# The transformed second MLP matrix of a transformer block: its column sums taken one step earlier, all six pairs staged through one ring of buffers, and the third block's x rows loaded earlier

## The chip, the cores and the metric

One core of a Trainium2 chip runs the whole program. The metric is device microseconds of one execution; lower is better. TensorE is called PE here and its weight loads PEld; DVE is VectorE, ACT is ScalarE, POOL is GpSimd, and SP is the queue of SyncE, which in this kernel only issues DMA transfers.

## What is computed

The reference is an attention layer followed by an MLP, on x of 2048 rows by 640 columns, in float32. Only the MLP is touched by the change:

```python
h = layernorm(x) * (1 + cb) + sb          # x is already the attention's output plus the input
h = h @ w1 + b1                           # 640 -> 1728
h = max(h, 0) ** 2
x = x + gb * (h @ w2 + b2)                # 1728 -> 640
```

## The kernel before, in words

**The MLP's loops.** The 2048 rows are eight blocks j = 0 to 7 of 256 rows (two halves of 128). The 1728 columns of w1 are 14 chunks of 128 (the last of 64), taken as seven pairs n = 0 to 6. A step (j,n) computes both chunks of a pair: `up` (L1145) multiplies the transposed, normalised rows `h` of the block by the chunk of w1 (15 matmuls into PSUM), ACT adds the bias and applies max(.,0) into the tile `ft` (L1162), DVE squares it (L1163). Products run in a split form of float32: a number is a high part `hi` (an ACT copy into a narrower type) and a low part `lo` (a DVE subtraction, L88), and a product is three matmuls, hi·hi, hi·lo, lo·hi, in that order. `split_a` (L1179) makes both parts of the squared tile into `ra`. The down product of a pair runs one step later than its `up`: its first half, down(0), after the first `up` of the next step, its second half, down(1), after the second `up`. So PE always needs the `ra` of the step before: ACT's copy for the first matmul of down(0), and DVE's low part for the third.

**Two forms of the down product.** In blocks 0 and 1 (`PLAIN` = 2) `down_plain` (L1295) multiplies with w2 as it is, held in the tiles `W2` (two per pair). From block 2 on `down_pair` (L1302) uses a scheme with seven products instead of eight, which wants sums of w2's quarters: for each of six pairs the combinations a, b and c (384, 256 and 384 columns wide), and one quarter that is overwritten in place, in `W2[2n][:, :, R]`. a, b and c live in DRAM (`TD`) and are fetched again by POOL for each block through a ring of four SBUF tiles (`ring`, L1217; `t_fetch`, L1267). Each fetched tile can be fetched into a ring place only after PE has used the one before it there.

**How the sums are made, in block 1.** For a pair, `t_load` (L1222) loads its two 128-row pieces of w2 into the rows `traw`; `t_sums` (L1228) is five DVE subtractions; `t_split` (L1241) is, for a, b, c and the kept quarter, an ACT copy and a DVE subtraction each, and SP's stores of a, b and c into `TD`. Pair p is loaded at the end of step (1,p), its sums stand at the end of step (1,p+1), its split in the first half of step (1,p+2), for p up to 3. Pair 4 is split at the end of (1,6). Pair 5 has its sums and its split in (2,2), in a place of its own: the tile of `h` that block 3 will use (`tst_end`).

**What sets the order.** PE, DVE, ACT and POOL run their instructions in the order in which the code issues them (`manual_schedule`, L1428), each engine in its own order; SP's order is chosen by the scheduler. Waits are by semaphores; an engine whose next instruction waits stands still. Rows of the tag `s1` (`traw`, the x rows `xx` of later blocks, the residual rows `xr`) come from five tiles, one of which holds a chunk of w1 for good, so four take turns: a new row's load waits until the last reader of the row before it in that tile is done.

**The layer norm of the next block.** While block j runs, `layer` (L1411) prepares block j+1 in pieces, at half-steps numbered 0 to 13 (2n and 2n+1): "load" (x rows), "add" (two DVE additions and SP's stores of the sums), "ln" (six ACT pieces; GpSimd works on the statistics after the second and the fourth), and the transposes with `hfb` and `h` at the numbers 8 to 12. The tables `LN_AT0` to `LN_AT2` and `LN_AT` (L1385) give the half-step of each; `LN_AT2` is for block 3, prepared during block 2.

The steps of which the prediction speaks, in the loop of L1430: m is 7j + n - 8.

Of the kernel before, what the change touches and what calls it, by code (L numbers as in the profile page):

```python
# [8 lines left out]
F32 = mybir.dt.float32  # L9
F32R = mybir.dt.float32r  # L10
I32 = mybir.dt.int32
AF = mybir.ActivationFunctionType
# [26 lines left out]
PLAIN = 2  # L39
# [12 lines left out]
def kernel(  # L52
# [19 lines left out]
    nc = tc.nc  # L72
# [14 lines left out]
    def lo(out_lo, full, hi, eng=None):  # L87
        (eng or nc.vector).tensor_tensor(out_lo, full, hi.bitcast(F32), op=ALU.subtract)  # L88
# [28 lines left out]
    def row(tag, name):  # L117
        return (pc if tag in ("s3", "s4") else mem).tile([P, D], F32, tag=tag, name=name, bufs=BUFS[tag])
# [7 lines left out]
    def ht(name, j, at=(32, 0)):  # L126

        t = mem.tile([P, NC * 512 + (32, 96)[j % 2]], F32R, tag=f"h{j % 2}", name=name, bufs=1)
        at = at[j % 2]
        return t[:, at : at + NC * 512].rearrange("p (d s n) -> p d s n", d=NC, s=2)  # L130
# [540 lines left out]
    for t in range(2, NT - 2):  # L671
        j, i = divmod(t, 2)
# [237 lines left out]
    W1, W2 = {}, {}  # L910
# [140 lines left out]
    for j in range(NB):  # L1051
        nxt = j + 1 < NB
        b, c = 2 * j + 5, 2 * j + 6
# [86 lines left out]
    NP = NF // 2  # L1140
# [29 lines left out]
    def plain(j, n):  # L1170
        return j < PLAIN or n == NF // 2 - 1 or j == NB - 1 and n >= NF // 2 - LAST
# [27 lines left out]
    def split_s(j, n):  # L1199
        t = FT[j, n]  # L1200
        a = RS[j, n] = p3.tile([P, 2, 4, P], F32, tag="rs", name=f"rs{j}_{n}").bitcast(F32R)
        nc.scalar.activation(a[:, 0], t[:, S1 : S4 + 1], AF.Copy)
        lo(a[:, 1], t[:, S1 : S4 + 1], a[:, 0])
# [7 lines left out]
    TD = [{r: dram.tile([P, 2, m], F32, name=f"td{n}_{r}") for r, m in RINGS.items()} for n in range(NP - 1)]  # L1211
    ITEMS = [(j, n, r) for j in range(PLAIN, NB) for n in range(NP) if not plain(j, n) for r in RINGS]
    L, R = slice(0, 384), slice(384, 640)
    TR_ = {}
    RING = {}

    def ring(r, name):  # L1217

        t = p3.tile([P, 768], F32, tag="ring", name=name, bufs=4)
        return t[:, : 2 * RINGS[r]].rearrange("p (s n) -> p s n", s=2).bitcast(F32R)  # L1220

    def t_load(n):  # L1222
        TR_[n] = [row("s1", f"traw{n}_{r}") for r in range(2)]
        for r in range(2):
            f = 2 * n + r
            nc.sync.dma_start(TR_[n][r], w2[f * P : (f + 1) * P])

    def t_sums(n):  # L1228
        a, b = TR_[n]
        l, r, m = slice(0, 256), slice(384, 640), slice(256, 384)  # L1230
        if n == NP - 2:
            TR_["end"] = ht("tst_end", 1).rearrange("p d s n -> p (d s n)")
            t = TR_["end"][:, :512].rearrange("p (s n) -> p s n", s=2)
        else:
            t = ring("b", f"tst{n}_b")
        TR_[n, "b"] = t
        for o, x, y in ((a[:, l], a[:, r], a[:, l]), (t[:, 1].bitcast(F32), b[:, r], a[:, r]),
                        (b[:, r], b[:, r], a[:, l]), (b[:, m], b[:, m], a[:, m]), (b[:, l], b[:, l], b[:, r])):
            nc.vector.tensor_tensor(o, x, y, op=ALU.subtract)

    def t_split(n):  # L1241

        a, b = TR_[n]
        for r, w in (("a", a[:, L]), ("b", TR_[n, "b"][:, 1].bitcast(F32)), ("c", b[:, L]), (None, b[:, R])):
            if r == "b":
                t = TR_[n, "b"]
            elif r and n == NP - 2:
                at = 512 if r == "a" else 1280
                t = TR_["end"][:, at : at + 768].rearrange("p (s n) -> p s n", s=2)
            else:  # L1250
                t = ring(r, f"tst{n}_{r}") if r else W2[2 * n][:, :, R]
            nc.scalar.activation(t[:, 0], w, AF.Copy)
            lo(t[:, 1], w, t[:, 0])
            if r:
                nc.sync.dma_start(TD[n][r], t.bitcast(F32))


    def plain_load(n):
# [60 lines left out]
    def add_bias(j, i):  # L1319
        add(XR[j, i], XR[j, i], bb)  # L1320
# [56 lines left out]
    def prep(n):  # L1377
        p_hi(n)
        p_lo(n)
        p_load(n)  # L1380
# [3 lines left out]

    LN_AT0 = {"load": 0, "add": (2, 4), "ln": (2, 4, 6, 6, 8, 8), 10: (0, 1), 11: (2, 3), 12: (4,)}  # L1385
    LN_AT1 = {"load": 3, "add": (5, 5), "ln": (5, 6, 6, 7, 8, 8), 9: (0, 1), 11: (2, 3), 12: (4,)}
    LN_AT2 = {"load": 4, "add": (6, 6), "ln": (7, 7, 8, 8, 9, 9), 10: (0, 1), 11: (2, 3), 12: (4,)}
    LN_AT = {"load": 0, "add": (3, 4), "ln": (4, 5, 6, 6, 7, 7), 8: (0, 1), 10: (2, 3), 12: (4,)}
    PREPS = iter([0, 4] * 5 + [0, 1])

# [20 lines left out]
    def layer(j, at):  # L1411
        todo = {1: LN_AT0, PLAIN: LN_AT1, PLAIN + 1: LN_AT2}.get(j, LN_AT)
        if j == NB:
            return
        if at in todo:
            t2(j, *todo[at])
        if todo["load"] == at:
            load_x1(j)
        for i in range(2):
            if todo["add"][i] == at:  # L1420
                add_x(j, i)
        for i in range(6):
            if todo["ln"][i] == at:
                if i == 0:
                    LN2[j] = ln_pieces(XM[j], f"b{j}", XX[j])
                next(LN2[j])
# [3 lines left out]
    for j in range(NB):  # L1430
        for n in range(NP):
            down = lambda k: prev and (down_plain if plain(*prev) else down_pair)(*prev, k)
            twice = not plain(j, n)
            m = NP * j + n - NP - 1
            done = j - 1 if j and prev else None
            up(j, 2 * n)
            if prev and not plain(*prev):
                split_s(*prev)
            down(0)
            if j < PLAIN:  # L1440
                layer(j + 1, 2 * n)
            if 0 < m < NP - 2:
                t_split(m - 1)
            if m == -1:
                t_load(0)
            if (j, n) == (PLAIN, 0):
                t_fetch(4)
            if j >= PLAIN:
                layer(j + 1, 2 * n)
            prep(next(PREPS, 0))  # L1450
            if n == 0 and j:
                if j - 1 >= PLAIN:
                    first_combos(j - 1)
                else:
                    Y[j - 1] = [row("s2", f"y{j - 1}_{i}") for i in range(2)]
                for r, i, c in (("2", 0, L), ("3", 0, R)):
                    end(j - 1, r, i, c)
            if n == 1 and j:
                gate(j - 1, 0)
                if j != PLAIN:  # L1460
                    finish(j - 1, j < PLAIN)
            if n == 1 and j == PLAIN:
                finish(j - 1, 0)
            if n == 2 and j == PLAIN:
                t_sums(NP - 2)
            if n == (2 if j > PLAIN else 1) and j:
                gate(j - 1, 1)
            if n == (5, 5, 4, 3)[min(j, 3)]:
                residual(j)
            for i in range(2):  # L1470
                if n == 6 and j == 0 or n == 5 and j >= PLAIN and i == 0:
                    add_bias(j, i)
            if j == NB - 1 and n == 1:
                for k in range(NP - LAST, NP - 1):
                    plain_load(k)
            if j == NB - 1 and n == 3:
                for k in range(NP - LAST, NP - 1):
                    plain_split(k)
            if j == NB - 1 and n == NP - 2:
                for i in range(2):  # L1480
                    by_gate(Y[j][i], Y[j][i], slice(0, D))
            if j == NB - 1 and n == NP - 1:
                split_a(j, n, (0,))
                for i in range(2):
                    add(Y[j][i], Y[j][i], XR[j, i])
            up(j, 2 * n + 1)
            if j >= PLAIN and n == 0:
                down(1)
            split_a(j, n, (0, 1) if (j, n) != (NB - 1, NP - 1) else (1,))
            if twice:  # L1490
                sums(j, n)
            if j < PLAIN or n:
                down(1)
            if m == NP + 1:
                t_split(NP - 2)
            prep(next(PREPS, 0))
            if n == 0 and j:
                end(j - 1, "4", 1, L)
                end(j - 1, "x", 1, R)
            if n == (2 if j > PLAIN else 1 if j == PLAIN else 0) and j:  # L1500
                finish(j - 1, j >= PLAIN)
            layer(j + 1, 2 * n + 1)
            if 0 <= m < NP - 2:
                t_sums(m)
            if m == NP - 2:
                t_split(m - 1)
            if 0 < m + 1 < NP - 1:
                t_load(m + 1)
            if m == NP - 1:
                for i in range(2):  # L1510
                    add_bias(j - 1, i)
            if j >= PLAIN and n == 5:
                add_bias(j, 1)
            if j == NB - 1 and n == NP - LAST:
                first_combos(j)
            prev = j, n
# [60 lines left out]
```

## Time and profile before

| | |
|---|---|
| time, median of 3 runs | 789.05 us (789.01 to 789.47) |
| the profiled execution | 788.85 us, of which the profile's span is 787.1 us |
| PE, DVE, ACT, POOL busy | 98%, 74%, 56%, 16% of the span |
| block 0 of the MLP begins | about 401 us |
| blocks 1, 2, 3, 4 begin (first `up`) | 448.92, 497.46, 546.82, 593.48 us |
| DMA in the stretch 495 to 543 us | 285 GB/s, engines busy 0.89 of the time |
| DMA in the stretch 590 to 636.6 us | 209 GB/s, engines busy 0.70 of the time |

A row of the timeline has the start, the duration, the engine, the source line, the operation, the tiles written and read, the shape and the number of merged instructions; at its end, in brackets, the idle time of the engine just before it and what ended that. Matmuls overlap, so a row of matmuls can end after the next one starts; the time from one row's start to the next's is what the row costs. The same holds, less strongly, on DVE and ACT. The profiled execution's own time has 1.75 us beside the span.

### The profile page before, as it was taken

To read this page: it belongs to the slowest core of one execution; us is meant where nothing else is said; L and a number is where in the kernel's file an instruction comes from. 1 tells how busy PE (TensorE), PEld (TensorE's weight loads), DVE (VectorE), ACT (ScalarE), POOL (GpSimd) and SP (SyncE) were. 2 spreads that over 40 slices of the span, in tenths; PEclk is the share of its full clock that TensorE was granted. 3 is DMA by queue.
4 is the path that set the end of the run, shared out by engine and by line. 5 is a ranking of instruction groups with operands and counts; after the bars stand their busy time and mean duration, and the time that the engine had idled before them with its cause. 6 is when DMAs were issued, how large, how long until landed. Compare 5 with 4: busy or idle time off the path is not lost.

```text
span 787.1 us, 15302 instructions
## 1 busy us (share of the span) xinstructions
PE 775.0 (98%) x5989; PEld 745.6 (95%) x5989; DVE 583.9 (74%) x1059; ACT 441.3 (56%) x988; POOL 124.3 (16%) x253
## 2 busy tenths in 40 slices
PE   9999999999999999999999999999999999999997
PEld 8899999999999889998999999999999999999997
DVE  6599899998788699986256666775757567585756
ACT  5766675475752365656766636455454645536331
POOL 3001101001000232320000001131131313213110
PEclk9999999999999999999999999999999999999999
DMA  9714244432120254222266365897675858657450
GB/s 336 281 59 139 83 152 156 134 113 89 68 102 1 83 169 168 84 100 85 101 194 209 101 208 207 289 319 229 177 221 167 266 149 264 204 169 211 117 168 34
DMA packets 50551, 126.03 MB, mean 160 GB/s; under 512 B 5991, under 2 KB 6759, under 8 KB 50479
## 3 DMA queue, kind: packets, MB, share of 16 engines
q1 hardware_dynamic: 33144, 83.99, 31.1%
q0 software_dynamic: 14752, 35.76, 16.3%
q10 hardware_dynamic: 2583, 5.30, 1.7%
q8 instruction: 47, 0.77, 0.4%
q14 instruction: 25, 0.20, 0.1%
HBM read 95.05 MB, written 29.88 MB: 159 GB/s over the span
## 4 chain that ended last, share of the span: by engine, by line
PE 82%; DVE 5%; DMA 5%; ACT 4%; issue 3%; POOL 1%; POOLq 0%; SPq 0%; ACTq 0%; DVEq 0%
PE up L78 19%; PE acc L78 14%; PE pwo L78 10%; PE pk L78 9%; PE pq L78 8%; PE pv L78 8%; PE acc3x L78 4%; PE kvp L440 3%; PE te L850 2%; DMA ring_b<-td_b 1%; PE numa L78 1%; DMA wm<-in_w_ss 1%; PE tb L359 1%; PE numc L78 1%; PE numb L78 1%
## 5 line engine op out<-in xcount | busy, mean ns | idle before, releaser
L78 PE MATMUL up<-h,w 128*128 128x256 f32 x1640 | 207.1, 278 | 0.4 <-ACT ft L1162 0.4
L78 PEld LDWEIGHTS up<-h,w 128*128 128x128 f32 x1640 | 196.3, 188 | 0.8 <-ACT ft L1162 0.6
L1162 ACT ACTIVATE ft<-up,b_t 128x256 f32<-128x256 f32 x104 | 48.8, 469 | 104.0 <-PE up L78 103.5
L78 PE MATMUL acc<-w,ra 128*128 128x384 f32 x452 | 100.1, 338 | 1.0 <-ACT ra L1186 1.0
L78 PE MATMUL pwo<-wo,ot 128*128 128x256 f32 (+3 forms) x512 | 81.1, 311 | 0.0
L1163 DVE TENSOR_TENSOR ft<-ft 128x256 f32<-128x256 f32 x104 | 44.0, 423 | 48.9 <-ACT ft L1162 47.2
L78 PE MATMUL pk<-wk,hT 128*128 128x384 f32 (+1 forms) x480 | 77.7, 312 | 0.2 <-ACT hT L371 0.2
L78 PEld LDWEIGHTS pwo<-wo,ot 128*128 128x128 f32 (+1 forms) x512 | 74.9, 188 | 2.7 <-issue 2.7
L78 PEld LDWEIGHTS acc<-w,ra 128*128 128x128 f32 x452 | 72.6, 188 | 4.1 <-DVE ra L88 2.8
L78 PE MATMUL pv<-wv,hT 128*128 128x384 f32 (+1 forms) x480 | 76.0, 309 | 0.0
L78 PE MATMUL pq<-wq,hT 128*128 128x384 f32 (+1 forms) x480 | 74.5, 311 | 0.4 <-ACT k L416 0.4
L78 PEld LDWEIGHTS pk<-wk,hT 128*128 128x128 f32 x480 | 71.8, 188 | 2.0 <-ACT hT L371 0.8
L78 PEld LDWEIGHTS pq<-wq,hT 128*128 128x128 f32 x480 | 70.6, 188 | 1.4 <-ACT k L416 0.9
L78 PEld LDWEIGHTS pv<-wv,hT 128*128 128x128 f32 x480 | 70.7, 188 | 0.4
L88 DVE TENSOR_TENSOR ra<-ft,ra 128x384 fp32r<-128x384 f32 (+2 forms) x86 | 36.8, 448 | 34.2 <-ACT ra L1186 21.5
L1186 ACT ACTIVATE ra<-ft 128x384 fp32r<-128x384 f32 x48 | 25.2, 525 | 32.6 <-DVE ft L1163 25.2
L88 DVE TENSOR_TENSOR h<-hfb,h 128x256 fp32r<-128x256 f32 x40 | 17.0, 425 | 35.1 <-ACT h L371 35.1
L78 PE MATMUL acc3x<-w,ra 128*128 128x256 f32 x248 | 43.0, 281 | 0.0
L78 PEld LDWEIGHTS acc3x<-w,ra 128*128 128x128 f32 x248 | 39.5, 188 | 1.6 <-DVE y L1327 1.4
L1272 POOL DMA_DIRECT2D ring_a<-td_a x34 | 18.3, 538 | 128.1 <-PE acc L78 107.4
L1177 DVE TENSOR_TENSOR ft<-ft 128x128 f32<-128x128 f32 x136 | 33.3, 286 | 1.2
L370 ACT ACTIVATE hfb<-tb,cols_b 128x256 f32<-128x256 f32 x40 | 22.5, 562 | 18.9 <-PE tb L359 11.3
(251 smaller groups left out, 1407.7 us busy)
## 6 DMA issues: line engine op xcount, KB each, us to landing
ring_c<-td_c POOLq DMA_DIRECT2D x34, 384.0 KB, 4.5
ring_a<-td_a POOLq DMA_DIRECT2D x34, 384.0 KB, 4.1
ring_b<-td_b POOLq DMA_DIRECT2D x34, 256.0 KB, 4.0
esp<-eq SPq DMA_DIRECT2D x12, 640.0 KB, 2.9
el<-esp SPq DMA_DIRECT2D x12, 640.0 KB, 3.9
rw<-in_w SPq DMA_DIRECT2D x23, 320.0 KB, 4.5
wm<-in_w_mod SPq DMA_DIRECT2D x20, 320.0 KB, 4.3
xb<-in_x SPq DMA_DIRECT2D x8, 640.0 KB, 4.0
```

The source lines that it names most:

```text
L78: nc.tensor.matmul(o, a, b, start=first and i == 0, stop=last and i == len(terms) - 1, skip_group_check=skip,)
L88: (eng or nc.vector).tensor_tensor(out_lo, full, hi.bitcast(F32), op=ALU.subtract)
L359: nc.tensor.transpose(p[:, i * P : (i + 1) * P], xn[:, i, d * P : (d + 1) * P], ident)
L370: nc.scalar.activation(hf, p[:, :256], AF.Identity, bias=cols[:, d : d + 1], scale=cols[:, 5 + d : 6 + d])
L440: nc.tensor.matmul(kvp[g // 4][64 * c : 64 * c + 64, a : a + 2 * n].rearrange("p (s n) -> p s n", s=2), v[:, u], e[:, :, o : o + n], start ...
L850: nc.tensor.transpose(p[:m, a : a + P], EU[2 * j + i][:, b : b + m], ident)
L1162: nc.scalar.activation(r, p, AF.Relu, bias=b1_t[:, f : f + 1])
L1163: nc.vector.tensor_tensor(r, r, r, op=ALU.mult)
L1177: nc.vector.tensor_tensor(t[:, o], t[:, a], t[:, b], op=op)
L1186: nc.scalar.activation(a[:, 0, :3], t[:, :3], AF.Copy)
L1272: nc.gpsimd.dma_start(RING[j, n, r], TD[n][r].bitcast(F32R))
```

## The change

For every pair: the load, the sums and the split of a, b and c stand one step earlier (load at the end of (1,p-1), pair 0 at the end of (0,6); sums at the end of (1,p); split in the first half of (1,p+1), in the order c, a, b). The kept quarter is taken out of the split and written by a function of its own, `t_keep`, in the first half of (1,p+2). Pairs 4 and 5 follow the same rule, so pair 5's sums stand in (1,5), its split in (1,6), its kept quarter in (2,0), and it uses the ring as the others do. The sum b is made in place in `traw` instead of in the ring tile. For block 3, `load` moves from half-step 4 to 1 of block 2, "add" from (6, 6) to (4, 5), the "ln" pieces from (7, 7, 8, 8, 9, 9) to (5, 6, 6, 7, 7, 8), and the first transposes from 10 to 9, the second from 11 to 10. The residual rows are loaded in step 6 instead of 5 of block 1, and in step 3 instead of 4 of block 2.

```diff
     def t_sums(n):
         a, b = TR_[n]
         l, r, m = slice(0, 256), slice(384, 640), slice(256, 384)
-        if n == NP - 2:
-            TR_["end"] = ht("tst_end", 1).rearrange("p d s n -> p (d s n)")
-            t = TR_["end"][:, :512].rearrange("p (s n) -> p s n", s=2)
-        else:
-            t = ring("b", f"tst{n}_b")
-        TR_[n, "b"] = t
-        for o, x, y in ((a[:, l], a[:, r], a[:, l]), (t[:, 1].bitcast(F32), b[:, r], a[:, r]),
+        for o, x, y in ((a[:, l], a[:, r], a[:, l]), (a[:, r], b[:, r], a[:, r]),
                         (b[:, r], b[:, r], a[:, l]), (b[:, m], b[:, m], a[:, m]), (b[:, l], b[:, l], b[:, r])):
             nc.vector.tensor_tensor(o, x, y, op=ALU.subtract)
     def t_split(n):
         a, b = TR_[n]
-        for r, w in (("a", a[:, L]), ("b", TR_[n, "b"][:, 1].bitcast(F32)), ("c", b[:, L]), (None, b[:, R])):
...
+        for r, w in (("c", b[:, L]), ("a", a[:, L]), ("b", a[:, R])):
+            t = ring(r, f"tst{n}_{r}")
             nc.scalar.activation(t[:, 0], w, AF.Copy)
             lo(t[:, 1], w, t[:, 0])
-            if r:
-                nc.sync.dma_start(TD[n][r], t.bitcast(F32))
+            nc.sync.dma_start(TD[n][r], t.bitcast(F32))
+    def t_keep(n):
+        t, w = W2[2 * n][:, :, R], TR_[n][1][:, R]
+        nc.scalar.activation(t[:, 0], w, AF.Copy)
+        lo(t[:, 1], w, t[:, 0])
-    LN_AT2 = {"load": 4, "add": (6, 6), "ln": (7, 7, 8, 8, 9, 9), 10: (0, 1), 11: (2, 3), 12: (4,)}
+    LN_AT2 = {"load": 1, "add": (4, 5), "ln": (5, 6, 6, 7, 7, 8), 9: (0, 1), 10: (2, 3), 12: (4,)}
             if j < PLAIN:
                 layer(j + 1, 2 * n)
-            if 0 < m < NP - 2:
-                t_split(m - 1)
-            if m == -1:
-                t_load(0)
+            if 0 < m < NP:
+                t_keep(m - 1)
+            if 0 <= m < NP - 1:
+                t_split(m)
...
-            if n == 2 and j == PLAIN:
-                t_sums(NP - 2)
-            if n == (5, 5, 4, 3)[min(j, 3)]:
+            if n == (5, 6, 3, 3)[min(j, 3)]:
                 residual(j)
...
-            if m == NP + 1:
-                t_split(NP - 2)
...
             layer(j + 1, 2 * n + 1)
-            if 0 <= m < NP - 2:
-                t_sums(m)
-            if m == NP - 2:
-                t_split(m - 1)
-            if 0 < m + 1 < NP - 1:
-                t_load(m + 1)
+            if 0 <= m + 1 < NP - 1:
+                t_sums(m + 1)
+            if 0 <= m + 2 < NP - 1:
+                t_load(m + 2)
```

More of the change, by code (lines that the diff above doesn't have):

```diff
@@ L1243, in t_split @@
         a, b = TR_[n]
-        for r, w in (("a", a[:, L]), ("b", TR_[n, "b"][:, 1].bitcast(F32)), ("c", b[:, L]), (None, b[:, R])):
[L1245 to L1251, printed above, removed]
+        for r, w in (("c", b[:, L]), ("a", a[:, L]), ("b", a[:, R])):
+            t = ring(r, f"tst{n}_{r}")
             nc.scalar.activation(t[:, 0], w, AF.Copy)
             lo(t[:, 1], w, t[:, 0])
-            if r:
-                nc.sync.dma_start(TD[n][r], t.bitcast(F32))
+            nc.sync.dma_start(TD[n][r], t.bitcast(F32))
[3 more added lines that the diff above has]
+        lo(t[:, 1], w, t[:, 0])
     def plain_load(n):
```

## The prediction

> **What bounds the kernel now.** I read the page's busy times first, then PE's timeline through blocks 1, 2 and 3, then the timelines of DVE, ACT and POOL beside the places where the change puts work, and last the landing times of the transfers.
>
> ```profile
> PE 775.0 (98%) x5989; PEld 745.6 (95%) x5989; DVE 583.9 (74%) x1059; ACT 441.3 (56%) x988; POOL 124.3 (16%) x253
> ```
>
> PE is the bound, and the change leaves its 5989 matmuls and their order alone. So all that can be gained is idle time of PE, and all that can be lost is new idle time of PE. PE's timeline of block 2, where the change takes work out, and of block 3, which has the same products and none of pair 5's work:
>
> ```profile
> 497.46 1.86 PE L78 MATMUL up<-h,w 128*128 128x256 f32 x15
> ...
> 523.44 1.86 PE L78 MATMUL up<-h,w 128*128 128x256 f32 x15
> ...
> 526.69 1.87 PE L78 MATMUL up<-h,w 128*128 128x256 f32 x15
> ...
> 531.48 0.61 PE L78 MATMUL acc<-ring_b,rs 128*128 128x256 f32 x3 [1.59 <-DMA ring_b<-td_b]
> 531.92 1.86 PE L78 MATMUL up<-h,w 128*128 128x256 f32 x15
> ...
> 543.75 1.42 PE L78 MATMUL up<-h,w 128*128 128x256 f32 x10 [0.37 <-ACT ft L1162]
> ...
> 546.82 1.86 PE L78 MATMUL up<-h,w 128*128 128x256 f32 x15
> ```
>
> ```profile
> 573.03 1.86 PE L78 MATMUL up<-h,w 128*128 128x256 f32 x15
> ...
> 586.94 1.93 PE L78 MATMUL up<-h,w 128*128 128x256 f32 x15
> ...
> 593.48 1.86 PE L78 MATMUL up<-h,w 128*128 128x256 f32 x15
> ```
>
> Block 2 takes 546.82 - 497.46 = 49.36 us. Without waits it would take the four first steps as they are (523.44 - 497.46 = 25.98), two steps with transposes as block 3 has them (586.94 - 573.03 = 13.91) and a last step (593.48 - 586.94 = 6.54): 46.43. The excess is **2.93 us**: step (2,4) takes 531.92 - 523.44 = 8.48 where the four steps before it took 25.98 / 4 = 6.50, so 1.98 there (1.59 of it the wait for `ring_b`), and 0.95 in the last two steps (the 0.37 is part of it). That is the most that block 2 can give back.
>
> **The change part by part.** All terms are added to the profiled execution, 788.85 us (787.1 of span and 1.75 beside it), which lies 0.20 under the median of the runs, 789.05; I carry no correction for that.
>
> *Recovered in block 2.* The transfers of this stretch and of block 3's, by the windows view, and the transfers of the first by the view of DMA issues:
>
> ```profile
> 495.00:543.00 48.00, 46.30 (x358) 45.58 (x357) 33.53 (x87) 25.04 (x56) 11.98 (x23) 1.00 0.89 285
> 590.00:636.60 46.60, 46.60 (x363) 45.91 (x363) 31.01 (x77) 24.04 (x52) 11.28 (x22) 1.00 0.70 209
> ```
>
> ```profile
> ring_b<-td_b POOLq DMA_DIRECT2D x6, 256.0 KB, 5.3
> ...
> traw<-in_w SPq DMA_DIRECT2D x2, 320.0 KB, 3.3
> ...
> x<-xm SPq DMA_DIRECT2D x2, 320.0 KB, 9.0
> ```
>
> The stretch moves 285 GB/s with the transfer engines busy 0.89 of the time; the stores `x<-xm` take 9.0 us to land. Pair 5's stores (384, 384 and 256 KB), its two `traw` rows and the x rows now go out mostly ahead of 503 us, before the ring is refetched at full pace, so the middle of block 2 comes near block 3's 0.70, where PE never waits for the ring. I take the whole excess back: **-2.93**. The bounds are 0 (no wait goes) and -2.93; if only the `ring_b` wait stays, -0.95 remains. What is late next in (2,4) is the third term below.
>
> *Sums one step sooner: the second row of pair 1.* A step has as many DVE and ACT operations as before (five sums, three parts, one kept quarter), so in the middle of block 1 nothing is added. But the order of the loads changes. `traw1_1` now takes the tile that `traw0_0` held, and its load on SP waits for DVE's last low part of pair 0 and stands behind the stores of c and a; its sums stand at the end of the same step. The rows of DVE around it, and the landing times (tile view of `traw` from 440 us, of the two rows ahead of that, and of `xx`):
>
> ```profile
> 461.01 0.42 DVE L1163 TENSOR_TENSOR ft<-ft 128x256 f32<-128x256 f32 x1 [2.18 <-ACT ft L1162]
> ...
> 462.71 0.42 DVE L1239 TENSOR_TENSOR traw<-traw 128x256 f32<-128x256 f32 x1
> 463.05 0.42 DVE L1239 TENSOR_TENSOR tst_b<-traw,traw 128x256 f32<-128x256 f32 x1
> ...
> 464.49 0.42 DVE L1163 TENSOR_TENSOR ft<-ft 128x256 f32<-128x256 f32 x1
> 464.90 0.56 DVE L88 TENSOR_TENSOR tst_a<-traw,tst_a 128x384 fp32r<-128x384 f32 x1
> ...
> 466.18 0.42 DVE L88 TENSOR_TENSOR w<-traw,w 128x256 fp32r<-128x256 f32 x1
> 467.85 0.43 DVE L1163 TENSOR_TENSOR ft<-ft 128x256 f32<-128x256 f32 x1 [1.25 <-ACT ft L1162]
> ```
>
> ```profile
> DMA to landing us min/median/max: 3.3/4.1/4.5
> ```
>
> ```profile
> DMA to landing us min/median/max: 2.8/3.1/3.3
> ```
>
> ```profile
> DMA to landing us min/median/max: 3.0/6.2/7.4
> ```
>
> DVE gets the five sums of pair 0 (1.78, 462.71 to 464.49 in the old place) and three low parts (464.90 to 466.18, 1.28) ahead of the square at 461.01: 3.06, of which 2.18 is idle time now, so the square comes at 461.9, and SP issues `traw1_1` at about 462.0. It lands at 462.0 + L. Four of the five sums read it (463.05 to 464.49: 1.44), then come the square and four low parts (464.49 to 466.18 and 0.34 more for the last: 2.03), then the square that now starts at 467.85. It starts at 465.5 + L. With L = 4.3 (between the median and the slowest of the busy rows) that is 469.8, **1.92 late**. Will PE feel it? PE wants the copy and low part of `ra` here, and ACT and DVE deliver them here:
>
> ```profile
> 477.40 0.68 PE L78 MATMUL acc<-w,ra 128*128 128x384 f32 x3
> ...
> 484.75 0.84 PE L78 MATMUL acc<-w,ra 128*128 128x384 f32 x3
> ```
>
> ```profile
> 476.32 0.53 ACT L1186 ACTIVATE ra<-ft 128x384 fp32r<-128x384 f32 x1 [0.71 <-DVE ft L1163]
> ...
> 477.67 0.19 ACT L1401 ACTIVATION_READ_ACCUMULATOR xx<-xm,smb 128x1 f32 x1
> ...
> 479.73 1.74 ACT L1408 ACTIVATE xm<-xm,nbb,sqb 128x640 f32<-128x640 f32 x2 [1.51 <-POOL nbb L1405]
> ...
> 483.98 0.53 ACT L1186 ACTIVATE ra<-ft 128x384 fp32r<-128x384 f32 x1 [0.71 <-DVE ft L1163]
> ```
>
> ```profile
> 484.53 0.76 DVE L88 TENSOR_TENSOR ra<-ft,ra 128x384 fp32r<-128x384 f32 x2 [0.59 <-ACT ra L1186]
> ```
>
> The late square delays the two additions for block 2's norm, those ACT's statistics, those the copies of the split, and so the next `ra`: each step hands the delay on. The copy of 476.32 is done at 476.85, 0.55 ahead of PE. At 484.53 there is no slack: the low part's first half is done at about 485.0, when PE wants it at 484.75 + 0.34 = 485.09, and PE's 0.84 instead of 0.68 shows that the group is already held up. So of the 1.92 about 0.07 is slack: **+1.85**, in general L - 2.45. Bounds: L = 2.8 (the quickest row) gives +0.35; L = 7.4 (the slowest x row) gives +4.95. The rows of pairs 2 to 5 wait likewise for the kept quarter, but their sums have cover: the split waits for ACT's norm anyway (the 1.51 above is POOL's), and then come the transposes.
>
> By the Trainium skill, "DMA: Bandwidth & Descriptors", section "Bandwidth", a transfer of 64 KB keeps the transfer engines 0.95 us and one of 1 MB 6.15 us (issued from GpSimd), which as an estimate puts a row of 328 KB at 2.3 us; this case's rows, 2.8 when alone and 4.1 in the median here, are longer, and I go by them. By the page's figure this term would be nothing and the sum 787.0.
>
> *Split of pair 5 ahead of the last relu of block 1.* In (1,6) four more ACT copies and four more DVE low parts (1.62) stand between the sums and the relu of the 64 columns:
>
> ```profile
> 496.72 0.42 DVE L1163 TENSOR_TENSOR ft<-ft 128x256 f32<-128x256 f32 x1
> ...
> 497.39 0.41 DVE L1167 TENSOR_TENSOR ft<-up,ft 64x256 f32<-64x256 f32 x1
> ...
> 498.17 0.98 DVE L88 TENSOR_TENSOR ra<-ft,ra 128x128 fp32r<-128x128 f32 x3
> ```
>
> ```profile
> 496.27 0.47 ACT L1166 ACTIVATE ft<-up,b_t 64x256 f32<-64x256 f32 x1
> ```
>
> ```profile
> 499.16 0.68 PE L78 MATMUL acc<-w,ra 128*128 128x384 f32 x3
> ```
>
> The copies need the last sum (496.8), take 1.1, so the relu ends at 498.4 and L1167 starts about 1.1 later; the first low part is done at 499.6, and PE wants it at 499.16 + 0.34 = 499.5. **+0.2**; bounds 0 and the 1.62 of the four low parts.
>
> *The earlier norm in block 2.* "ln" now puts the fifth piece directly behind the fourth on ACT, with POOL's three operations between them, and the next relu is queued behind it:
>
> ```profile
> 523.06 0.53 ACT L1186 ACTIVATE ra<-ft 128x384 fp32r<-128x384 f32 x1 [0.49 <-DVE ft L1163]
> ```
>
> The fourth piece follows this copy, from 523.49, and takes 0.91 (0.72 and 0.19): 524.40. From the end of that piece to the norm it is 479.73 - 477.86 = 1.87 in block 1: 526.27. Half of the 1.74 and the relu (0.47) end at 527.5, and PE's second `up`, which now waits for that relu since both share a PSUM tile, is due at 526.69: **+0.85**. Bounds 0 (POOL quicker, or `up` late already) and 1.9. Behind the relu wait DVE's square and PE; nothing else does.
>
> *At nothing:* the sum b in place (same operation); the residual rows one step later in block 1 (their first reader is in block 2); the transposes one half-step earlier (the same matmuls); block 3's x rows at 1 instead of 4 (their tile is free after (2,0), their reader at 4). If that cover goes, the additions on DVE wait for a row, some 1 us, as rival three says of rows in general.
>
> Sum: 788.85 + 1.85 + 0.2 + 0.85 - 2.93 = **788.8 us**.
>
> **The rivals.**
> 1. *Nothing of the new waits shows except (1,6).* `traw1_1` is quick (2.8, as the lone rows were: +0.35) and the relu in (2,4) is hidden: 788.85 + 0.35 + 0.2 - 2.93 = 786.5. For it: the two rows loaded ahead of block 1 landed that quickly. Against: the rows inside block 1 didn't, and POOL's 1.87 is an order that no transfer changes. With no cost at all, 785.9.
> 2. *Quick row, but the wait in (2,4) as computed:* 786.5 + 0.85 = 787.3.
> 3. *Late row (slower).* SP's queue ahead of `traw1_1` (two stores of 384 KB) makes it land as late as the x rows, 6.2: +3.75, and 788.85 + 3.75 + 0.2 + 0.85 - 2.93 = 790.7; at 7.4 it is 791.9. It decides from L = 6.1 on. Against it: the `traw` rows so far never took over 4.5.
> 4. *The change doesn't do what it says:* `ring_b` stays late, because its fetch waits for PE to free the tile and the path is still full. 788.85 + 1.85 + 0.2 + 0.85 - 0.95 = 790.8.
>
> **How the numbers follow.** 0.2%, about what a measurement can tell, is 1.58 us: faster is below 787.47, slower above 790.63. Forecast 0.33 (same); rival 1 0.21 (faster, 0.02 of it with no cost); rival 2 0.11 (on the edge: 0.05 faster, 0.06 same); rival 3 0.22 (slower); rival 4 0.13 (on the edge: 0.10 slower, 0.03 same). Faster 0.26, same 0.42, slower 0.32. The range runs from just under rival 1 (786.2) to rival 3 with a row between 6.2 and 7.4 (791.6); outside are rival 1 without costs and the slowest row.
>
> **What would show it.** Right: DVE waits for `traw` in (1,1) for 2 us and more; the copies of `ra` near 476.32 and 483.98 come 1.9 later; block 1 is 1.9 us longer; no `ring_b` wait in (2,4), but PE's second `up` there waits for ACT; block 2 at 47.3 us. Wrong: no DVE wait for a row, and block 1 as long as before (rival 1 or 2); a row over 6 us (rival 3); a `ring_b` wait of over 1 us (rival 4); or waits of PE in a step not named here.

## The result, and the profile after

The changed kernel takes 790.46 us (median of 21 runs, 789.22 to 791.58), the kernel before 789.05 us (median of 21, 787.51 to 791.72). The ratio is **1.0016, 95% interval 1.0009 to 1.0023**: slower by 1.3 us, 0.16%. The forecast was 788.8 us, 0.03 under the profiled execution of the kernel before, that is, no change. The time lies in the stated range and in the band of 0.2% that was called same, but the kernel got slower where the sum had it unchanged. The difference is small because a gain of 2.9 us and costs of 4.5 us nearly cancel.

The profiled execution has a span of 787.6 us (787.1 before). The busy times on its page hardly differ:

```profile
PE 775.5 (98%) x5989; PEld 745.2 (95%) x5989; DVE 584.8 (74%) x1059; ACT 441.9 (56%) x988; POOL 124.6 (16%) x253
```

Where the time went is seen in PE's timeline of blocks 1 and 2, in the rows that begin a block or a longer step and in those that wait:

```profile
447.90 1.86 PE L78 MATMUL up<-h,w 128*128 128x256 f32 x15
...
470.53 1.03 PE L78 MATMUL acc<-w,ra 128*128 128x384 f32 x3 [0.82 <-ACT ra L1186]
...
478.62 1.04 PE L78 MATMUL acc<-w,ra 128*128 128x384 f32 x3 [0.70 <-ACT ra L1186]
```

```profile
499.06 1.86 PE L78 MATMUL up<-h,w 128*128 128x256 f32 x15
...
501.87 0.44 PE L78 MATMUL acc<-w,ra 128*128 128x384 f32 x1 [0.53 <-DVE ra L88]
...
503.25 1.86 PE L78 MATMUL up<-h,w 128*128 128x256 f32 x15
...
525.88 1.86 PE L78 MATMUL up<-h,w 128*128 128x256 f32 x15
...
530.10 2.03 PE L78 MATMUL up<-h,w 128*128 128x256 f32 x15 [0.79 <-ACT ft L1162]
...
533.20 0.51 PE L78 MATMUL acc<-ring_b,rs 128*128 128x256 f32 x3
...
547.41 1.86 PE L78 MATMUL up<-h,w 128*128 128x256 f32 x15
```

Of the kernel before, the rows that the prediction did not show:

```profile
448.92 1.86 PE L78 MATMUL up<-h,w 128*128 128x256 f32 x15
...
500.70 1.97 PE L78 MATMUL up<-h,w 128*128 128x256 f32 x15
```

Block 1 took 497.46 - 448.92 = 48.54 us then, and takes 499.06 - 447.90 = 51.16 now: **+2.62**. This sits in two places, those of the two waits above: from the first `up` of (1,3) to its second it is 4.80 us, and in (1,4) 4.66, where both were 3.42. Block 2 takes 547.41 - 499.06 = 48.35, where it took 49.36. In it two stretches are longer than before: the first `up` to the second of (2,0), 503.25 - 499.06 = 4.19 against 500.70 - 497.46 = 3.24 (**+0.95**), and in (2,4) 530.10 - 525.88 = 4.22 against 3.25 (**+0.97**). Without these two the block would take 46.43, which is the stall-free length that the prediction worked out: the **2.93 us have come back in full**, and the row of `ring_b` at 533.20 has no wait in brackets. The sum is 2.62 + 0.95 + 0.97 - 2.93 = +1.61. The medians differ by 1.41. The spans differ by 0.5 only because the profiled execution of the changed kernel came to block 1 about 1.0 us sooner. About half of that, 0.54, stood already when block 0 began (400.38 against 400.92); nearly all the rest, 0.47, comes from the stretch around PE's wait for `ra` in block 0 (432.30 to 437.30, 5.00 us, against 5.47), which took between 4.40 (e9_split1) and 5.47 us among the executions below. Nothing before block 1 differs between the kernels but one load in the last step of block 0, so this is put down to the execution and not to the change.

The transfers of the middle of block 2, by the windows view from 504 to 536 us, the changed kernel first and the kernel before second:

```profile
504.00:536.00 32.00, 31.21 (x245) 30.89 (x245) 19.43 (x48) 14.96 (x31) 9.79 (x19) 1.00 0.89 274
```

```profile
504.00:536.00 32.00, 30.41 (x237) 30.15 (x237) 22.57 (x56) 15.70 (x34) 9.99 (x20) 1.00 0.98 320
```

The transfer engines were busy nearly all the time (0.98) and are so no longer (0.89).

The two waits in block 1 have their origin earlier, in DVE's timeline of (1,1) and (1,2), and on SP:

```profile
460.08 0.42 DVE L88 TENSOR_TENSOR tst_b<-traw,tst_b 128x256 fp32r<-128x256 f32 x1
...
461.15 0.42 DVE L1163 TENSOR_TENSOR ft<-ft 128x256 f32<-128x256 f32 x1
...
466.21 1.09 DVE L1233 TENSOR_TENSOR traw<-traw,traw 128x256 f32<-128x256 f32 x3 [2.96 <-DMA traw<-in_w]
...
469.51 0.42 DVE L1163 TENSOR_TENSOR ft<-ft 128x256 f32<-128x256 f32 x1
```

```profile
459.81 0.33 SPq L993 DMA_DIRECT2D xx<-in_x  x1
460.24 0.38 SPq L1242 DMA_DIRECT2D td_c<-tst_c  x1
460.71 0.39 SPq L1242 DMA_DIRECT2D td_a<-tst_a  x1
461.20 0.61 SPq L1226 DMA_DIRECT2D traw<-in_w  x1
```

```profile
DMA to landing us min/median/max: 4.9/4.9/4.9
```

The last line is the landing time of the load issued at 461.20 (tile view of `traw`, that instruction alone). DVE stands still for 2.96 us until it lands. From the third `up` of block 1 (454.16; 455.18 before) to the square of the second half of (1,2) it is 469.51 - 454.16 = 15.35 us, where it was 467.85 - 455.18 = 12.67: **2.68 late**. A table under e5_early sets this lateness beside the length of block 1.

### The profile page after: what moved, and what is told of

The parts are those of the page before. It is cut to its first block, busy times and chain, and to the rows that moved or that the text cites. A ratio compares the mean times of both kernels' runs of the same rounds, so it can differ in the third digit from the quotient of the medians.

```text
span 787.6 us, 15310 instructions
## 1 busy us (share of the span) xinstructions
PE 775.5 (98%) x5989; PEld 745.2 (95%) x5989; DVE 584.8 (74%) x1059; ACT 441.9 (56%) x988; POOL 124.6 (16%) x253
## 5 line engine op out<-in xcount | busy, mean ns | idle before, releaser
L1162 ACT ACTIVATE ft<-up,b_t 128x256 f32<-128x256 f32 x104 | 48.9, 471 | 97.0 <-PE up L78 96.5
```

The costliest lines, as they stand in the source:

```text
L1162: nc.scalar.activation(r, p, AF.Relu, bias=b1_t[:, f : f + 1])
```

## Experiments

My theory after the result: three separate costs (the late second row of pair 1; pair 5's split ahead of the last square of block 1; ACT's wait for POOL in (2,4)) and one gain (pair 5's transfers out of the middle of block 2). Its rivals: that DVE's earlier work, not the row, makes block 1 longer; that the row is late whenever it is issued, as the path is busy; that the norm of block 3 and not W2's part brought the gain. Ratios are to the kernel before, run alongside; steps are read from one profiled execution of each.

**e1_row: the row's tile free sooner, the load ahead of the stores.** In step (1,1) the last addition of block 0's end goes ahead of the split of pair 0:

```diff
-            if 0 <= m < NP - 1:
+            if 0 < m < NP - 1:
                 t_split(m)
...
                 if j != PLAIN:
                     finish(j - 1, j < PLAIN)
+                if m == 0:
+                    t_split(m)
```

> The changed kernel with one move: in step (1,1) the last addition of block 0's end (y + xr, second half) stands before the split of pair 0 instead of behind it, so that the second row of pair 1 takes that xr row's tile and its load is issued ahead of the stores of c and a. Same instructions. Theory (the late row makes block 1 longer): the row is issued about 1.5 us sooner and lands about 2.2 us sooner; DVE's wait for it falls from 2.96 to under 1 us, PE's waits for ra in (1,3) and (1,4) (0.82 and 0.70) go, block 1 falls from 51.2 to about 49.0 us, and the time to about 788.3. Rival (the five sums and the three low parts that DVE does earlier, or the new order of the split, make block 1 longer): block 1 stays at 51 us and the time at 790.4. Second rival (the row is late because the path is busy, not because it is issued late): it lands as late as now, and nothing changes.

Measured: 788.58 us, ratio 1.0000 (0.9991 to 1.0010). DVE's wait fell to 2.13 us, not to under 1: the row was issued only 0.6 us sooner against block 1's start, as SP stood ahead of it at the load of x rows, which waited for a store to land. The square was 1.77 late (469.18 less 454.74, less 12.67), and block 1 took 50.28, 1.74 longer than before. So the direction holds and the size does not; the mechanism was tried again in e5_early.

```profile
465.62 1.09 DVE L1233 TENSOR_TENSOR traw<-traw,traw 128x256 f32<-128x256 f32 x3 [2.13 <-DMA traw<-in_w]
...
469.18 0.42 DVE L1163 TENSOR_TENSOR ft<-ft 128x256 f32<-128x256 f32 x1
```

**e2_split5: pair 5's split behind the last relu.**

```diff
-            if 0 <= m < NP - 1:
+            if 0 <= m < NP - 2:
                 t_split(m)
...
             if j < PLAIN or n:
                 down(1)
+            if m == NP - 2:
+                t_split(m)
```

> The changed kernel with the split of pair 5 moved, in step (1,6), from ahead of the last relu to behind that step's second down product. Theory (four low parts of 1.6 us stand ahead of the last square of block 1 and make PE wait in (2,0)): three of the four go behind it, L1167 comes 1.3 us sooner, PE's 0.53 wait for the low part in (2,0) goes, the first step of block 2 falls from 4.19 to about 3.3 us, time about 789.6. Rival (block 1 is late as a whole, and (2,0) only shows it): the wait stays, time 790.4.

Measured: the wait in (2,0) is gone and the stretch falls from 4.19 to 3.42 us, as expected. The time doesn't show it: 789.42 us, ratio 1.0014 (1.0005 to 1.0024), which neither separates it from the changed kernel nor excludes 0.8 us. In its profiled execution the row went out later still, 7.61 us after the third `up` of block 1 against 7.04 in the changed kernel; DVE waited 3.53 for it, PE in (1,3) 1.40, and block 1 took 51.74.

**e3_norm: a relu between the fourth and the fifth piece of the norm.**

```diff
-    LN_AT2 = {"load": 1, "add": (4, 5), "ln": (5, 6, 6, 7, 7, 8),
+    LN_AT2 = {"load": 1, "add": (4, 5), "ln": (5, 6, 6, 7, 8, 8),
```

> The changed kernel with the fifth piece of block 3's norm at half-step 8 instead of 7, so that a relu stands between the fourth piece and the fifth on ACT. Theory (ACT waits for POOL's statistics with the relu behind it): PE's 0.79 wait for ACT in (2,4) goes, that part of the step falls from 4.22 to 3.25 us, time about 789.5. Rival (the wait only moves to the transposes, which need the norm half a step later): PE waits 0.5 us and more for xm before the transposes, time 790.4.

Measured: the stretch in (2,4) falls from 4.22 to 3.26, block 2 to 47.31; no wait came up at the transposes. 788.75 us, ratio 0.9993 (0.9980 to 1.0007). The rival falls.

**e4_all: the three moves together.**

> The three moves together. Theory (the three costs are separate and add up, the 2.93 us recovered in block 2 stay): 790.4 - 2.2 - 0.9 - 0.9 = about 786.4, block 1 at 49.0 and block 2 at 46.5 us. Rival (they hide one another, or the ring wait comes back when block 2 is quicker): 788 and more, with a wait for ring_b, ring_a or ring_c in block 2.

Measured: 786.84 us, ratio **0.9978** (0.9969 to 0.9987), block 1 50.32, block 2 46.65. The steps add up, and block 2 keeps what it recovered. Block 1 is 1.8 over what it was, as in e1_row, and not at the 49.0 expected.

**e5_early: the row loaded sooner still.** The last addition of block 0's end, and its store, go to the end of (1,0), ahead of the sums:

```diff
-                if j != PLAIN:
-                    finish(j - 1, j < PLAIN)
+                if j > PLAIN:
+                    finish(j - 1, 0)
...
                 finish(j - 1, j >= PLAIN)
+                if j < PLAIN:
+                    finish(j - 1, 1)
```

> The changed kernel with the last addition of block 0's end and its store at the end of step (1,0), ahead of the sums of pair 0: the xr row's tile comes free some 3 us sooner, and the second row of pair 1 is loaded into it ahead of the x rows and of all stores of sums. Same instructions. Theory (block 1 is longer only by the wait for this row): the row is issued at about 10 us after block 1's start instead of 13.3, DVE does not wait for it any more (2.96 in the changed kernel, 2.13 in e1_row), block 1 falls from 51.2 to 48.7 us, as before the change, and the time is 1.2 us under the kernel before. Rival (the row is only part of it; the work of the sums and the split at new places costs the rest): DVE's wait goes, but block 1 stays above 50 us and the time over that of the kernel before.

Measured: 788.34 us, ratio 0.9990 (0.9980 to 1.0000): 0.8 us under the kernel before by the ratio, where 1.2 was expected, and the interval reaches up to no difference. The row was issued 1.7 us sooner against block 1's third `up` than in the changed kernel (I had expected 3; DVE's addition and the issue of the store ahead of it took the rest) and landed in 4.1 instead of 4.9. DVE's wait is 0.46, but ACT now waits where it did not:

```profile
464.44 1.09 DVE L1233 TENSOR_TENSOR traw<-traw,traw 128x256 f32<-128x256 f32 x3 [0.46 <-DMA traw<-in_w]
...
468.58 0.42 DVE L1163 TENSOR_TENSOR ft<-ft 128x256 f32<-128x256 f32 x1
```

```profile
466.74 0.53 ACT L1240 ACTIVATE tst_a<-traw 128x384 fp32r<-128x384 f32 x1 [0.32 <-DMA td_c<-tst_c]
467.77 0.42 ACT L1240 ACTIVATE tst_b<-traw 128x256 fp32r<-128x256 f32 x1 [0.50 <-DMA td_a<-tst_a]
```

The four ring tiles carry three parts of each pair, so pair 1's a and b wait until pair 0's c and a have been stored. That wait stood behind the row's and becomes visible when the row is quick. The square is 13.68 - 12.67 = 1.01 late, and block 1 takes 49.53, 0.99 longer than before: neither the 48.7 of the theory nor the 50 and more of the rival.

Put side by side, the lateness of that square and the extra length of block 1 agree within 0.06 us:

| kernel | DVE's wait for the row | square late by | block 1 | longer than 48.54 by |
|---|---|---|---|---|
| before | none | 0 | 48.54 | 0 |
| e5_early | 0.46 | 1.01 | 49.53 | 0.99 |
| e1_row | 2.13 | 1.77 | 50.28 | 1.74 |
| changed | 2.96 | 2.68 | 51.16 | 2.62 |

The other kernels that split pair 1 ahead of this square follow the same line: e2_split5 is 3.25 late and 3.20 longer, e3_norm 3.08 and 3.07, e6_w2only 3.07 and 3.05, e4_all 1.78 and 1.78, e12_no_split5 0.96 and 0.96, e8_best 0.73 and 0.72, e11_best_again 0.60 and 0.59. So the changed kernel's 2.62 is the lowest of four executions with this block 1 (2.62 to 3.20).

The work of sums and split at their new places is thus not the whole cost: e5_early does it in the same steps, and 1.6 of the 2.6 us are gone. For the last 1.0 the place of the split does matter, as e9_split1 and e10_late_splits show. The rival that the row can't be quicker falls.

**e6_w2only and e7_lnonly: the two parts of the change alone.** e6_w2only is the changed kernel with

```diff
-    LN_AT2 = {"load": 1, "add": (4, 5), "ln": (5, 6, 6, 7, 7, 8), 9: (0, 1), 10: (2, 3), 12: (4,)}
+    LN_AT2 = {"load": 4, "add": (6, 6), "ln": (7, 7, 8, 8, 9, 9), 10: (0, 1), 11: (2, 3), 12: (4,)}
...
-            if n == (5, 6, 3, 3)[min(j, 3)]:
+            if n == (5, 6, 4, 3)[min(j, 3)]:
```

and e7_lnonly is the kernel before with the opposite edit of these lines ((5, 5, 4, 3) becoming (5, 5, 3, 3)).

> The changed kernel with block 3's norm (its loads, additions, pieces and transposes) and block 2's residual rows where they were before the change: only the part on W2 is left. Theory (the ring wait went because pair 5's rows and stores left block 2): no ring wait in (2,4), no wait for the relu there either, the 0.95 us in the last two steps of block 2 are back; block 2 as long as in the changed kernel, 48.3 us, block 1 51.2, time 1.3 us over the kernel before. Rival (it went because the x rows of block 3 come sooner): the wait for ring_b of about 1.6 us is back, time 3 us over.

> The kernel before with only the other part: block 3's norm and block 2's residual rows at the changed places, W2's sums as before. Theory: block 1 stays at 48.5 us; pair 5's stores are still in block 2, so a ring wait stays there, and the wait of ACT for POOL comes on top of it or is hidden by it: block 2 49.4 to 50.4 us, time 0 to 1 us over the kernel before. Rival (the earlier norm alone takes the ring wait away): block 2 47.4 us, time 2 us under.

Measured: e6_w2only 790.05 us, ratio 1.0013 (1.0003 to 1.0024); block 1 51.59, block 2 48.24. No ring wait, no relu wait in (2,4), and the last steps of block 2 have their 0.37 wait and some 0.9 us again. By the steps, the norm's part gives 0.95 there and takes 0.97 in (2,4), so the time comes out as the changed kernel's. e7_lnonly 788.26 us, ratio 0.9992 (0.9980 to 1.0005), not told from the kernel before; block 1 48.54, block 2 48.85 (under the 49.4 to 50.4 expected), with a wait of PE for ACT of 1.08 in (2,4) and no wait for the ring. The transfers say which part freed the path (windows view, 504 to 536 us, e6_w2only first):

```profile
504.00:536.00 32.00, 32.00 (x252) 31.98 (x251) 20.12 (x50) 14.65 (x30) 9.74 (x19) 1.00 0.92 283
```

```profile
504.00:536.00 32.00, 30.82 (x234) 29.71 (x233) 22.19 (x56) 16.79 (x37) 9.73 (x19) 1.00 1.00 322
```

The `ring_b` of (2,4), by the tile view of that fetch alone, in the kernel before and in e6_w2only:

```profile
DMA to landing us min/median/max: 8.4/8.4/8.4
```

```profile
DMA to landing us min/median/max: 5.4/5.4/5.4
```

With W2's part alone the path falls to 283 GB/s and this fetch lands 5.4 us after its issue, in the changed kernel 4.9. With the norm's part alone the path stays full and the fetch takes 7.0; no wait shows, but PE, 2.2 us behind by then (1.08 of it the wait for ACT), comes 1.4 us after it has landed, so without that lag PE would have wanted it about when it landed. The Trainium skill, "DMA: Bandwidth & Descriptors", section "Issuing engines are not separate DMA queues", says that transfers issued by different engines run on the same 16 engines and interleave; this case's traces agree: a fetch that POOL issues got 3.0 us quicker when pair 5's rows and stores, which SP issues, left its stretch (e6_w2only), and 3.5 us with the norm's transfers moved too (the changed kernel).

**e8_best and e11_best_again: e5_early with the moves of e2_split5 and e3_norm.**

> The early addition of e5_early with the moves of e2_split5 and e3_norm. Theory (three separate costs, and the 2.93 us recovered stay): block 1 48.7, block 2 46.5 us, time 3.3 us under the kernel before. Rival: as e4_all, 1.8 us under, because something else holds block 1 at 50 us.

> e8_best once more, for its wait in (2,1): there ring_a landed 5.45 us after its fetch, against 4.61 in e4_all, which splits pair 5 at the same place and had no such wait. If the late split of pair 5 makes the fetch late, the wait is there again and the step from the second to the third up of block 2 takes over 4 us; if the landing was a chance of that execution, it takes 3.3 us. Time 2.5 to 3.3 us under the kernel before.

Measured: 786.25 us, ratio **0.9963** (0.9950 to 0.9976), and again 786.11 us, ratio **0.9972** (0.9961 to 0.9984). This is 2.9 and 2.2 us under the kernel before, with both intervals clear of it, and under the changed kernel. It is less than the 3.3 expected: block 1 took 49.26 and 49.13 instead of 48.7, as ACT still waits 0.43 and 0.42 us for a store of pair 0. In the first execution one step of block 2 was 0.97 longer, with this row of PE:

```profile
510.25 0.77 PE L78 MATMUL acc<-ring_a,rs 128*128 128x384 f32 x3 [0.68 <-DVE y L1319]
```

The profile names a DVE addition, but the product also waits for `ring_a`, which landed 5.5 us after its fetch, 0.1 us before PE went on. It is `ring_a` that PE waited for: in e4_all, e11_best_again and e12_no_split5 this product starts while the same addition still runs (509.02 in e11_best_again, the addition from 508.96 to 509.77). In the second execution the fetch took 4.9 us, the step 3.26, block 2 46.58. So one of two executions of this kernel had the wait; the margin is small.

**e9_split1: pair 1's split out of the square's way.**

```diff
-            if 0 <= m < NP - 1:
+            if 0 <= m < NP - 1 and m != 1:
                 t_split(m)
...
+            if m == 1:
+                t_split(m)
             if 0 <= m + 1 < NP - 1:
                 t_sums(m + 1)
```

> e5_early with the split of pair 1 moved, in step (1,2), from ahead of the step's second square to behind the two additions of the norm. In e5_early ACT waits there for the stores of pair 0 to land (0.32 and 0.50 us) before it may write the ring tiles again, and DVE's square, which PE's next ra needs, stands behind. Theory (what is left of block 1's extra time, 1.0 us, is how late this square is): the square comes at its old distance from block 1's start, PE's wait in (1,4) (0.44) goes, block 1 falls by 0.9 us to 48.6, time 0.8 us under e5_early, some 1.3 us under the kernel before. Rival (the wait for the ring moves to pair 2, whose split then waits for pair 1's later stores): block 1 stays at 49.5 us, with waits of ACT or DVE for td stores in (1,3).

Measured: 788.15 us, ratio 0.9995 (0.9985 to 1.0005), no better than e5_early. The square of (1,2) is on time (467.16 - 454.49 = 12.67), yet PE's wait in (1,4) stays (0.43) and block 1 is 49.48. My expectation failed, and not by its rival: no ring wait came up. The three ACT copies now stand between the pieces of the norm, whose third piece (L1393) starts 18.76 us after the third `up`, where it was 17.70 before the change, and ACT's copy for the next `ra` comes 22.23 after it, as in e5_early (22.24), against 21.14 before the change. So a late square lengthens block 1, but it is not the only thing that can.

**e10_late_splits: all splits of pairs 1 to 5 there, with e3_norm.**

> e5_early with the splits of pairs 1 to 5 all moved to that place of their steps (behind the norm's pieces, ahead of the next sums), and the fifth piece of block 3's norm at half-step 8 as in e3_norm. Theory (costs in block 1 arise only where work stands ahead of the square that PE's ra needs): block 1 48.6 us or less, (2,0) without a wait, block 2 46.5 us, time 3.3 us under the kernel before. Rival (late stores hold the ring tiles, and block 2's first fetches are late, as ring_a was in e8_best): a wait of 0.7 us and more for ring_a in (2,1), or waits for td stores in block 1; time 2.4 us under, as e8_best.

Measured: 787.89 us, ratio 0.9990 (0.9981 to 0.9998). Block 1 falls to 48.09, 0.45 under what it was before the change, but block 2 rises to 49.30. The place in (2,0) was expected to have no wait, and PE waits 0.76 there for the relu (L1162); the larger part is this:

```profile
508.45 0.79 PE L78 MATMUL acc<-ring_c,ra 128*128 128x384 f32 x3 [1.36 <-DMA ring_c<-td_c]
```

The rival was right in kind, with `ring_c` in the place of `ring_a`: this fetch went out 4.6 us after block 2's start, in e11_best_again 0.5 us before it, and landed after 7.3 us instead of 4.1. That the later stores hold the ring tile fits this, but is not shown: the profile names a load of residual rows as what released the fetch.

**e12_no_split5: e8_best with pair 5's split back.**

> e8_best with the split of pair 5 back at the place that the changed kernel gives it, ahead of the last relu of block 1. Theory (the place costs 0.95 us in (2,0), and the ring's first fetch gains nothing from it): the wait of 0.53 in (2,0) is back, no wait for ring_a in (2,1), time 0.9 us over a kernel that has no wait in (2,1), and as e8_best if the wait in (2,1) is regular.

Measured: 787.15 us, ratio 0.9977 (0.9964 to 0.9990); the wait in (2,0) is back (0.54). e11_best_again, run alongside, is 1.0 us quicker by the medians, but the intervals overlap, so the time alone does not show it; the step does: 4.17 us from the first `up` of (2,0) to the second against 3.39. No wait for `ring_a` came up in (2,1).

## Why the prediction was right or wrong

**Block 2's recovery (-2.93): right** in size, and in part for the reason given. The 46.43 is what is left when the two new costs are taken off; the kernels without these costs come to 46.65 (e4_all) and 46.58 (e11_best_again). Of the 2.93, W2's part brought the 1.98 of step (2,4): e6_w2only shows that it frees the path, e7_lnonly that the earlier norm does not. The 0.95 of the last two steps came from the earlier norm (it is lost again in e6_w2only), for which the prediction gave no reason of its own. And the path did not come near block 3's 0.70: over 495 to 543 us it is busy 0.86 of the time (263 GB/s), and PE has no wait for the ring even so.

**The earlier norm in (2,4) (+0.85): right**, 0.97; the forecast's own terms (526.27 + 0.87 + 0.47, less 526.69) give 0.92. The way there was a little different: ACT waits for POOL twice in the changed kernel, 0.99 ahead of the third piece and then 1.60 ahead of the fifth, with the relu behind it:

```profile
524.05 0.83 ACT L1393 ACTIVATE xx<-xm,smb 128x640 f32<-128x640 f32 x1 [0.99 <-POOL smb L1390]
...
528.76 0.92 ACT L1400 ACTIVATE xm<-xm,nbb,sqb 128x640 f32<-128x640 f32 x1 [1.60 <-POOL nbb L1397]
529.59 0.45 ACT L1162 ACTIVATE ft<-up,b_t 128x256 f32<-128x256 f32 x1
```

**The second row of pair 1 (+1.85): the mechanism was right, the size was not.** The step that failed is "With L = 4.3": L was 4.9. The rule L - 2.45 gives 2.47 for 4.92, and 2.62 was measured. The other 0.15 fits a slip in the step before, "SP issues `traw1_1` at about 462.0", which took the row to wait for DVE's last low part of pair 0. That part was done at 460.50, but SP issued the row at 461.20: it went without a gap from the load of x rows, which had waited 1.2 us for a store to land (459.81), over the two stores. Counted from the third `up` it is 7.04 us instead of the 6.82 computed, and 7.31 to 7.61 in e2_split5, e3_norm and e6_w2only; in all four the row follows that x load by 1.37 to 1.39 us.

As to L, I took a value between the median and the slowest `traw` row of the trace before (4.1 and 4.5), though I had written that this row goes out right behind two stores. In e2_split5, e3_norm and e6_w2only, which leave this place as it is, it took 4.9, 5.0 and 5.0 us, so 4.9 is no accident. PE also felt it in a place that the forecast did not look at: it followed the delay to (1,4) and (1,5), but the `ra` made from the late square is needed in (1,3), and the longer stretches are there and in (1,4) (+1.38 and +1.24). The rival with the late row (6.2) named a row that lands late behind the two stores, and overshot. The estimate of 2.3 us for such a row, worked out beside the forecast from the Trainium skill, "DMA: Bandwidth & Descriptors", section "Bandwidth", was further from the 4.9 than any of the rows beside it.

**Pair 5's split in (1,6) (+0.2): wrong**, 0.95. The step that failed is "the relu ends at 498.4 and L1167 starts about 1.1 later". I let L1167 wait for ACT's relu alone. It also stands behind all four low parts on DVE itself. DVE's rows in the changed kernel:

```profile
498.48 0.42 DVE L1163 TENSOR_TENSOR ft<-ft 128x256 f32<-128x256 f32 x1
...
499.15 0.42 DVE L88 TENSOR_TENSOR w<-traw,w 128x256 fp32r<-128x256 f32 x1
499.48 0.55 DVE L88 TENSOR_TENSOR tst_c<-traw,tst_c 128x384 fp32r<-128x384 f32 x1
499.95 0.55 DVE L88 TENSOR_TENSOR tst_a<-traw,tst_a 128x384 fp32r<-128x384 f32 x1
500.42 0.42 DVE L88 TENSOR_TENSOR tst_b<-traw,tst_b 128x256 fp32r<-128x256 f32 x1
500.75 0.41 DVE L1167 TENSOR_TENSOR ft<-up,ft 64x256 f32<-64x256 f32 x1
```

From the square to L1167 it is 2.27 us, where it was 0.67 (496.72 to 497.39): the full 1.6 of the four low parts, the upper bound that I had written down and set aside. The first low part of `ra` was thus due at 498.17 + 1.6 + 0.33 = 500.1 instead of 499.6, 0.6 behind PE; 0.16 more is that the sums end later against block 2's start, which makes the 0.77 by which the part comes late (501.87 - 499.06 = 2.81 us after the start, against 2.04). The remaining 0.18 falls in the rest of that half and was not taken apart. e2_split5 takes three of the four out of the way and the stretch loses 0.77.

**The sum.** The two mis-sized terms are 0.77 and 0.75 too small, (2,4) 0.12; together 1.64, which is the whole distance from the forecast (-0.03) to what the steps show (+1.61). At nothing I had put the other edits, and no step shows a cost of theirs.

**What stays open.** e10_late_splits makes block 1 0.45 shorter than before the change, with the same instructions. By PE's timeline this sits in (1,5) and (1,6), in two stretches that were held up a little before (3.77 to 3.61 and 4.03 to 3.74 us; the `ra` groups of 0.84 and 0.86 us at 484.75 and 492.30 are 0.69 now); which of the moved operations had held them was not taken apart. A version with block 1 of e10_late_splits and block 2 of e11_best_again would by their lengths be a further 1.0 us quicker than the latter (49.13 - 48.09), unless the late splits exclude it; it wasn't tried. And what makes the row of pair 1 slower to land behind its two stores than other rows of block 1, some of which also follow stores, stays open.

## What to carry to other kernels

When work is moved ahead of an instruction that the bound engine needs, add up everything that now stands ahead of it on its own engine as well as on the engine that releases it, and take the later of the two: here the order on DVE alone gave 1.6 us, and the forecast set it aside as an upper bound. When a load is moved so that it waits for a tile's last reader, look also at what its own queue must issue first, and what that waits for; and take the slow end of the rows in the trace for its landing (4.5 here, 4.9 measured). And when a wait is taken away, look at once for the next resource of the same step, here the ring tiles behind the row.

## What the runs showed of the hardware that was not expected

The load of the same row of 320 KB landed 4.1 to 5.0 us after its issue, depending on where it stood: 4.1 to 4.6 right behind one store (4.1 in e5_early, 4.6 in e12_no_split5), 4.2 and 4.4 right behind a load of x rows (e4_all, e1_row), 4.9 and 5.0 behind that load and two stores of 384 KB (the changed kernel and e2_split5, e3_norm and e6_w2only). Stores of 384 KB into DRAM took 5.3 and 5.8 us there (e5_early), long enough to hold back the tile that they read from. Executions of unchanged code differ by several tenths: PE's wait for `ra` near 435 us, in block 0, was 0.26 in e1_row and 1.02 in e12_no_split5. Where ACT went from the fourth piece of the norm straight to the fifth, it stood idle for GpSimd's three small operations for 1.60 or 1.61 us in each of six executions (the changed kernel, e1_row, e2_split5, e5_early, e7_lnonly, e9_split1).
